# Layer 2 of the first expert placed between the parts of its layer 1, the first sigmoid one step later, and a pad tile, in an mLSTM cell followed by hash-routed experts

## The chip, the cores and the metric

The kernel runs on one core of one Trainium2 chip. The metric is the time of one execution on the device, in microseconds (us). Before the change three runs gave 402.64, 405.05 and 405.24 us; the median is 405.05 us. The engines are PE (matmul), ACT, DVE and POOL, and SP, whose queue issues most transfers.

## The reference

Two blocks follow each other, all in fp32. The first is an mLSTM cell over 4 batches, 8 heads, 768 positions and head dimension 40; the kernel computes it in chunks of 128 positions. The second sends each of the 3072 resulting rows of 320 numbers to one of 8 experts, picked by a hash of its token.

```python
m_new = np.maximum(f_gate[:, :, t] + m, i_gate[:, :, t])
f_stab = np.exp(f_gate[:, :, t] + m - m_new)
i_stab = np.exp(i_gate[:, :, t] - m_new)
C = f_stab[..., None, None] * C + i_stab[..., None, None] * np.einsum('bhd,bhe->bhde', vt, kt)
n = f_stab[:, :, None] * n + i_stab[:, :, None] * kt
o = 1.0 / (1.0 + np.exp(-o_gate[:, :, t]))
y[:, :, t] = o * np.einsum('bhde,bhe->bhd', C, qt) / np.maximum(np.abs(nq), 1.0)
...
x = attn_out.transpose(0, 2, 1, 3).reshape(B * S, H * D)
expert_idx = token_ids * np.int64(2654435761) % np.int64(E)
for e in range(E):
    xe = x[expert_idx == e]
    out[expert_idx == e] = np.maximum(xe @ w1[e], 0.0) @ w2[e]
```

## The kernel before

**Stage 1** runs 24 steps, s = 0 to 23, one for each batch and chunk of 128 positions. All instructions are written out by hand in the order in which each engine runs them (`manual_schedule`), so an engine that waits holds up everything behind it. In step s the SP queue issues the gate rows R of step s+3, k and q of step s+5, v of step s+4, then the o-gate tiles that the table `o_at` (L658) puts into this step, and last the stores of finished rows to `x_rows` (`waiting`). k and q lie in six buffers each, `[128, 8, 64]` in fp32, of which 40 of every 64 numbers are loaded: one 160-byte piece for each partition and head, 256 bytes apart. v lies in rows of 164 bytes, og in rows of 160 bytes that follow each other without a gap. Each of these loads carries 160 KB.

On PE a step begins with the transposes of k and q of step s+2 (`turn`, L321), then come scores (L368), decays (L332), the state (L399) and the output (L420, L426). ACT takes the exponentials (L336) and copies (dec L346, add L403, kT and qT L322). The output gate is taken for eight tiles at once: `sig_at` (L656) puts three sigmoids behind steps 6, 12 and 17, each a table load, an activation over 2560 columns, and a table load back (L360, L336). The sigmoid reads eight og tiles, so it waits for the last of these eight loads, and the next exponentials wait behind it. In the step after a sigmoid the copies of kT and qT go to DVE. After a sigmoid POOL multiplies two tiles a step by their gate (L443, `gated`), and SP stores them one or two steps later (L766).

**Stage 2** works off the experts in order. Layer 1 (`layer1`, L841) goes through eight blocks of hidden units in four pairs; each block gives a tile `mh` in PSUM (four buffers), which DVE or ACT turns into h by a relu (L864, L866). Layer 2 (`layer2`, L882) gives for each of three row tiles a tile `zp` (L886), which ACT copies (L819) and POOL scatters to the output (L820). The rows of an expert are gathered by POOL (L108), transposed on PE (L833, L835), and copied to xT by DVE or ACT (L839, L837). A fourth, shared tile xr holds 32 remainder rows of each of four experts; its transposed form remT is copied by POOL into the last 32 columns of xT (L919).

For expert 0 layer 1 is split. Its first two row tiles are gathered and transposed within stage 1 (`early_turn`), and part 1 runs over their 256 columns (L956). Then come the third tile and the remainder (`turns(0)[2:]`, L957), then part 2 over columns 256 to 416 (L959), then the three tiles of layer 2 (L961). The weights of expert 0 are loaded in slices by SP in steps 17 to 23; those of experts 1 and 2 (W1 and W2, 2.5 MB each) are issued from ACT's queue by `one` (L944) within part 2, and those of the later experts by SP.

Of the kernel before, what the change touches and what calls it, by code (L numbers as in the profile page):

```python
# [8 lines left out]
F32 = mybir.dt.float32  # L9
# [8 lines left out]
P = 128  # L18
# [4 lines left out]
def kernel(  # L23
# [66 lines left out]
    def weights(src1, src2, wpool, w2pool, eng=None):  # L90
# [10 lines left out]
        return w1t, w1c, w2t  # L101

    xg0 = early.tile([P, NJ, DB * P], F32, name="xg0")
    xT0 = early.tile([P, DB, CAP], F32, name="xT0")
# [39 lines left out]
    with tc.tile_pool(name="gates", bufs=1) as gp, \  # L144
# [481 lines left out]
        def route_index():  # L626
# [18 lines left out]
            2: [lambda: route_iotas(0)], 3: [lambda: route_iotas(1), route_consts, route_parts], 4: [route_experts],  # L645
            5: [route_chosen], 8: [route_extra, route_masked], 9: [route_rank], 10: [route_slots], 11: [route_places],
            21: [route_index], 22: [route_tiles],
# [6 lines left out]
        for i, part in enumerate(slices_of(0)):  # L654
            pieces.setdefault((17, 18, 19, 20, 21, 22, 23)[i], []).append(part)
        sig_at = {6: 0, 12: 1, 17: 2}  # L656
        o_at = {}
        for i, j in enumerate((2, 2, 3, 3, 4, 4, 5, 5, 6, 7, 8, 8, 9, 10, 10, 11, 12, 13, 13, 14, 15, 15, 16, 16)):  # L658
            o_at.setdefault(j, []).append(i)
# [61 lines left out]
        for s in range(NT):  # L721
# [43 lines left out]
            for i in range(2):  # L765
                if ndone < s and ndone // NG <= nsig and s - 1 not in sig_at:  # L766
                    gated(ndone)
                    waiting.setdefault(min(s + 1 + (s < NT - B - 1), NT), []).append(ndone)
                    ndone += 1
# [111 lines left out]

    def layer2(w, h, n, idx, apart, between=lambda j: None):  # L882
        for j in range(n):
            zp = mps.tile([P, Dm], F32, name="zp")
# [11 lines left out]
    with tc.manual_schedule():  # L896
# [38 lines left out]
        for e in range(E):  # L935
# [8 lines left out]
            def one(_):  # L944
                if ahead:
                    ahead.pop(0)()
                if e == 0 and len(W) < 3:
                    load_weights(len(W), nc.scalar)

# [5 lines left out]
            if e == 0:  # L955
                layer1(W[0], xT0, h, 0, 2 * P)  # L956
                for piece in turns(0)[2:]:  # L957
                    piece()
            layer1(W[e], xTs[e], h, 2 * P if e == 0 else 0, CAP, one)  # L959
            nc.gpsimd.tensor_copy(hrem[g][:, i], h[:, :, NM:])  # L960
            layer2(W[e], h, NJ, cols_of(s_idx, e * NJ), True, after)  # L961
            if e + 3 < E:
# [3 lines left out]
    with tc.If(nx > 0):  # L966
        with tc.For_i(0, nx, 1) as k:
# [13 lines left out]
            layer1(w, xT, h, 0, P)  # L981
            layer2(w, h, 1, lambda j: gs[:, 1:2], False)

# [29 lines left out]
```

## Time and profile before

| | before |
|---|---|
| median of 3 runs | 405.05 us (402.64 to 405.24) |
| profiled execution, its own time | 406.89 us |
| its span, first to last instruction | 405.0 us |
| mean granted TensorE clock (1 is full) | 0.971 |
| PE busy | 372.7 us, 92% |
| DVE, ACT, POOL busy | 34%, 28%, 36% |
| share of the chain that ended last: PE, POOL, DMA | 66%, 9%, 6% |

The span is the time on the chip's engines; the profiled execution's own time lies 1.9 us above it. PE is busy in most of the span in both stages, but matmuls are pipelined and their busy time also grows when the clock falls, so single waits are read from the timeline. A DMA share of 1.00 means that the 16 DMA engines have, on average, something under way all the time.

### The profile page before, as it was taken

The numbers are of one execution on the slowest core, as the hardware profiler recorded it, in microseconds if no ns is written. First come the engines' busy times: TensorE is split into PE (matmuls) and PEld (weight loads), VectorE is DVE, ScalarE is ACT, GpSimd is POOL, SyncE is SP. The second block draws the span as 40 slices with busy tenths as digits, with TensorE's granted clock in tenths as the row PEclk, the third lists the DMA queues.
The fourth block names the chain that finished last, engine by engine and source line by source line (L and its number), as shares of the span: only waits on it lengthen the run. The fifth ranks groups of instructions, "written<-read, shape, count | busy, mean of one in ns | idle before, by whom it ended". The sixth has DMA issues, their size and how long they took to land.

```text
span 405.0 us, 7980 instructions
## 1 busy us (share of the span) xinstructions
PE 372.7 (92%) x3211; PEld 260.8 (64%) x3211; DVE 138.6 (34%) x355; ACT 113.0 (28%) x232; POOL 144.0 (36%) x247
## 2 busy tenths in 40 slices
PE   8598896999998878799999999999999999999992
PEld 7487774878887765676565575556565575575561
DVE  8646765697786852110201201101201201101100
ACT  5366446558557421111111101201110101101100
POOL 8342424887996446113115023013115021010020
PEclk9789996999999999699999999999999999999998
DMA  9799999999999943897183192053182000000000
GB/s 124 107 157 125 149 160 148 158 188 160 159 171 203 265 157 99 270 362 245 32 235 106 32 275 81 20 182 128 32 252 93 14 16 31 2 32 16 2 18 31
DMA packets 124220, 51.02 MB, mean 126 GB/s; under 512 B 104338, under 2 KB 120174, under 8 KB 124182
## 3 DMA queue, kind: packets, MB, share of 16 engines
q1 hardware_dynamic: 116614, 36.73, 46.0%
q0 software_dynamic: 2496, 8.20, 6.5%
q10 hardware_dynamic: 5072, 5.57, 4.6%
q8 instruction: 26, 0.43, 0.5%
q14 instruction: 12, 0.10, 0.1%
HBM read 42.10 MB, written 8.71 MB: 125 GB/s over the span
## 4 chain that ended last, share of the span: by engine, by line
PE 66%; POOL 9%; issue 6%; DMA 6%; DVE 6%; ACT 5%; POOLq 0%; SPq 0%; DVEq 0%; ACTq 0%
PE zp L886 22%; PE mh L857 21%; PE mh L850 6%; PE tr L321 3%; PE sp L368 3%; DMA R<-gate_pieces 2%; PE xh L426 2%; POOL xg L108 2%; ACT og L360 2%; PE ab L332 2%; POOL x L443 1%; PE tp L833 1%; DVE w L374 1%; PE xh L420 1%; PE zp L927 1%
## 5 line engine op out<-in xcount | busy, mean ns | idle before, releaser
L886 PE MATMUL zp<-w2t,h 128*128 128x320 f32 x384 | 105.2, 433 | 0.0
L857 PE MATMUL mh<-xT,w1t 128*128 128x416 f32 (+2 forms) x288 | 98.6, 488 | 3.9 <-POOL xT L919 2.6
L886 PEld LDWEIGHTS zp<-w2t,h 128*128 128x128 f32 x384 | 72.7, 190 | 31.8 <-issue 2.9
L857 PEld LDWEIGHTS mh<-xT,w1t 128*128 128x128 f32 x288 | 52.6, 195 | 42.6 <-issue 38.0
L820 POOL DMA_INDIRECT out_dram<-zo,s_idx x26 | 25.6, 985 | 93.1 <-ACT zo L819 93.1
L839 DVE COPY xT<-tp 128x384 f32<-128x384 f32 x15 | 8.4, 558 | 139.1 <-PE tp L835 99.5
L866 ACT ACTIVATE h<-mh 128x416 f32<-128x416 f32 (+2 forms) x36 | 17.2, 478 | 113.3 <-PE mh L850 60.5
L864 DVE TENSOR_SCALAR h<-mh 128x416 f32<-128x416 f32 (+2 forms) x36 | 19.6, 543 | 60.1 <-PE mh L850 29.0
L819 ACT COPY zo<-zp 128x320 f32<-128x320 f32 x26 | 11.1, 425 | 101.6 <-PE zp L886 93.4
L374 DVE TENSOR_TENSOR w<-sp,w 128x512 f32<-128x512 f32 x48 | 30.8, 683 | 18.6 <-ACT w L336 18.6
L426 PE MATMUL xh<-v,w 128*64 128x41 f32 x768 | 34.8, 223 | 0.0
L336 ACT ACTIVATE w<-ab 128x512 f32<-128x512 f32 x48 | 26.0, 594 | 20.5 <-PE ab L332 17.9
L960 POOL COPY hrem<-h 128x256 f32<-128x256 f32 x8 | 3.2, 398 | 79.3 <-ACT h L866 79.3
L368 PE MATMUL sp<-qT,kT 64*128 64x128 f32 x384 | 30.4, 297 | 1.0 <-DVE w L374 0.9
L426 PEld LDWEIGHTS xh<-v,w 128*64 128x64 f32 x768 | 30.8, 139 | 0.1
L368 PEld LDWEIGHTS sp<-qT,kT 64*128 64x128 f32 x384 | 25.5, 199 | 5.4 <-issue 3.0
L850 PE MATMUL mh<-xT,w1c 64*128 64x416 f32 (+2 forms) x144 | 28.1, 509 | 0.4 <-DVE h L864 0.4
L108 POOL DMA_INDIRECT xg<-x_rows,g_idx x24 | 23.4, 974 | 13.2 <-issue 6.4
L420 PE MATMUL xh<-C,qs 128*64 128x82 f32 x320 | 27.4, 250 | 0.0
L409 POOL TENSOR_TENSOR C<-C,add 64x164 f32<-64x164 f32 x32 | 17.6, 551 | 26.9 <-ACT add L403 25.7
L321 PE MATMUL tr<-ident,q 128*128 128x128 f32 x96 | 15.8, 290 | 8.9 <-ACT dec L346 6.5
L443 POOL TENSOR_TENSOR x<-x,og 128x320 f32<-128x320 f32 x24 | 20.5, 872 | 5.4 <-DVE x L439 5.4
(188 smaller groups left out, 392.9 us busy)
## 6 DMA issues: line engine op xcount, KB each, us to landing
w2t<-in_moe_w_dram SPq DMA_DIRECT2D x5, 1280.0 KB
w1t<-in_moe_w_dram SPq DMA_DIRECT2D x5, 1024.0 KB
k<-in_k_dram SPq DMA_DIRECT2D x24, 160.0 KB
v<-in_v_dram SPq DMA_DIRECT2D x24, 160.0 KB
og<-in_o_gate_dram SPq DMA_DIRECT2D x24, 160.0 KB
x_rows<-x SPq DMA_DIRECT2D x24, 160.0 KB
q<-in_q_dram SPq DMA_DIRECT2D x23, 160.0 KB
w2t<-in_moe_w_dram ACTq DMA_DIRECT2D x2, 1280.0 KB
```

The source lines that it names most:

```text
L108: nc.gpsimd.indirect_dma_start(out=xg, out_offset=None, in_=x_d[:rows, :], in_offset=bass.IndirectOffsetOnAxis(ap=idx, axis=0),)
L321: nc.tensor.transpose(tp[:, j, :], d[what][:, 2 * j : 2 * j + 2, :].rearrange("p h d -> p (h d)"), ident[:])
L336: nc.scalar.activation(w[:, hf], ab[:], AF.Exp)
L368: nc.tensor.matmul(sp[hf][:, j, :], lhsT=d["kT"][r, j, :], rhs=d["qT"][r, j, :], start=True, stop=True)
L374: nc.vector.tensor_tensor(d["w"][:, hf], d["sp"][hf][:], d["w"][:, hf], op=ALU.mult)
L420: nc.tensor.matmul(xh[t, 2 * j : 2 * j + 2, :], lhsT=d["qs"][:, j, t], rhs=Cs[b][c % 2][:, j].rearrange("p h d -> p (h d)"), start=True, s ...
L426: nc.tensor.matmul(hs[t, 2 * j + hf, :], lhsT=d["w"][:, hf, j, t], rhs=d["v"][:, 2 * j + hf, :], start=(c == 0), stop=True, skip_group_che ...
L443: nc.gpsimd.tensor_tensor(x[:], x[:], og[s // NG][:, s % NG], op=ALU.mult)
L820: ins = nc.gpsimd.indirect_dma_start(out=out[:, :], out_offset=bass.IndirectOffsetOnAxis(ap=idx, axis=0), in_=zo[:], in_offset=None, bound ...
L850: nc.tensor.matmul(hp[i][:, : c1 - c0], lhsT=w1c[r, fp, :], rhs=xT[r, 2, c0:c1], start=first, stop=not first,)
L857: nc.tensor.matmul(hp[i][:, : c1 - c0], lhsT=w1t[:, db, fb * P : (fb + 1) * P], rhs=xT[:, db, c0:c1], start=(first and db == 0), stop=(not ...
L886: nc.tensor.matmul(zp[:], lhsT=h[:, fb, j * P : (j + 1) * P], rhs=w[2][:, fb, :], start=(fb == 0), stop=(fb == FB - 1),)
```

## The change

1. **Pad.** A tile of 128 bytes for each partition stands ahead of xg0 in the pool `early`. All that is laid out behind it moves by 128 bytes: xg0, xT0, h0, and the buffers of stage 1 and of stage 2. The first of the k and q buffers begin 224 bytes behind a multiple of 256 before and 96 bytes behind one after; with heads 256 bytes apart this holds for each of their 160-byte pieces. Before, a piece therefore has 32 bytes ahead of the next multiple and 128 behind it; after, it ends at the multiple. Of og's eight pieces in a row four cross such a multiple before and after.
2. **First sigmoid.** `sig_at` puts it behind step 7 instead of 6, and the first eight og loads move one step later. The routing pieces of step 8 move to step 7. Gating starts one step later, and rows are always stored in the step after their gating, so that tiles 8 and up are stored one step earlier than before.
3. **Layer 2 of expert 0.** Its tiles 0 and 1, whose columns of h are complete after part 1, now run behind part 1; the third row tile and the remainder are transposed between them (behind tile 0). The loads of W1 and W2 are issued on ACT within part 1.

```diff
+    early.tile([P, 32], F32, name="pad")
     xg0 = early.tile([P, NJ, DB * P], F32, name="xg0")
...
-            5: [route_chosen], 8: [route_extra, route_masked], 9: [route_rank], 10: [route_slots], 11: [route_places],
+            5: [route_chosen], 7: [route_extra, route_masked], 9: [route_rank], 10: [route_slots], 11: [route_places],
...
-        sig_at = {6: 0, 12: 1, 17: 2}
+        sig_at = {7: 0, 12: 1, 17: 2}
         o_at = {}
-        for i, j in enumerate((2, 2, 3, 3, 4, 4, 5, 5, 6, 7, 8, 8, 9, 10, 10, 11, 12, 13, 13, 14, 15, 15, 16, 16)):
+        for i, j in enumerate((3, 3, 4, 4, 5, 5, 6, 6, 7, 8, 8, 9, 9, 10, 10, 11, 13, 13, 14, 14, 15, 15, 16, 16)):
...
-                    waiting.setdefault(min(s + 1 + (s < NT - B - 1), NT), []).append(ndone)
+                    waiting.setdefault(s + 1, []).append(ndone)
...
-    def layer2(w, h, n, idx, apart, between=lambda j: None):
-        for j in range(n):
+    def layer2(w, h, js, idx, apart, between=lambda j: None):
+        for j in js:
...
             def one(_):
                 if ahead:
                     ahead.pop(0)()
-                if e == 0 and len(W) < 3:
-                    load_weights(len(W), nc.scalar)
...
-                layer1(W[0], xT0, h, 0, 2 * P)
-                for piece in turns(0)[2:]:
-                    piece()
+                layer1(W[0], xT0, h, 0, 2 * P, lambda fp: len(W) < 3 and load_weights(len(W), nc.scalar))
+                third = turns(0)[2:]
+                layer2(W[0], h, range(2), cols_of(s_idx, 0), True, lambda j: j == 0 and [piece() for piece in third])
             layer1(W[e], xTs[e], h, 2 * P if e == 0 else 0, CAP, one)
...
-            layer2(W[e], h, NJ, cols_of(s_idx, e * NJ), True, after)
+            layer2(W[e], h, range(2 if e == 0 else 0, NJ), cols_of(s_idx, e * NJ), True, after)
```

PE between the two stages before, from the end of part 1 (128x256) over part 2 (128x160) to layer 2 of expert 0 (xT_72 is xT0, h_73 is h0):

```order
L850 MATMUL mh<-xT_72,w1c 128x256 x4
L857 MATMUL mh<-xT_72,w1t 128x256 x4
L833 MATMUL tp<-ident,xg_71 128x128 x2
L835 MATMUL tp<-ident,xg_71 128x128
L833 MATMUL tp<-ident,xr 128x128 x2
L835 MATMUL tp<-ident,xr 128x128
L857 MATMUL mh<-xT_72,w1t 128x160 x4
...
L850 MATMUL mh<-xT_72,w1c 128x160 x4
L857 MATMUL mh<-xT_72,w1t 128x160 x4
L886 MATMUL zp<-w2t,h_73 128x320 x24
```

The same place after (names one higher, lines shifted by one):

```order
L851 MATMUL mh<-xT_73,w1c 128x256 x4
L858 MATMUL mh<-xT_73,w1t 128x256 x4
L887 MATMUL zp<-w2t,h_74 128x320 x8
L834 MATMUL tp<-ident,xg_72 128x128 x2
L836 MATMUL tp<-ident,xg_72 128x128
L834 MATMUL tp<-ident,xr 128x128 x2
L836 MATMUL tp<-ident,xr 128x128
L887 MATMUL zp<-w2t,h_74 128x320 x8
L858 MATMUL mh<-xT_73,w1t 128x160 x4
...
L851 MATMUL mh<-xT_73,w1c 128x160 x4
L858 MATMUL mh<-xT_73,w1t 128x160 x4
L887 MATMUL zp<-w2t,h_74 128x320 x8
```

Eight matmuls of layer 2 now stand ahead of the transposes and eight between them and part 2; eight are left behind part 2.

ACT at the same place before; the relus of 256 columns are part 1, those of 160 part 2:

```order
L665 COPY xT_72<-tpx 128x3x128 x2
L866 ACTIVATE h_73<-mh 128x256 x4
L837 COPY remT<-tp 128x384
L96 DMA w1t<-in_moe_w_dram 128x2x1024
L99 DMA w1c<-in_moe_w_dram 64x4x128 x2
L100 DMA w2t<-in_moe_w_dram 128x8x320
L866 ACTIVATE h_73<-mh 128x160 x2
```

And after:

```order
L666 COPY xT_73<-tpx 128x3x128 x2
L96 DMA w1t<-in_moe_w_dram 128x2x1024
L99 DMA w1c<-in_moe_w_dram 64x4x128 x2
L100 DMA w2t<-in_moe_w_dram 128x8x320
L867 ACTIVATE h_74<-mh 128x256 x2
L96 DMA w1t<-in_moe_w_dram 128x2x1024
L99 DMA w1c<-in_moe_w_dram 64x4x128 x2
L100 DMA w2t<-in_moe_w_dram 128x8x320
L867 ACTIVATE h_74<-mh 128x256 x2
L820 COPY zo<-zp 128x320
L838 COPY remT<-tp 128x384
```

Both weight loads have moved ahead of relus of part 1, the first of them ahead of all.

SP in steps 15 and 16 before, up to the last two o-gate tiles:

```order
L192 DMA v_101<-in_v_dram 128x8x40
L188 DMA og<-in_o_gate_dram 128x8x40 x2
L202 DMA R_122<-gate_pieces 6x2x1024
L192 DMA k_91<-in_k_dram 128x8x40
L192 DMA q_96<-in_q_dram 128x8x40
L192 DMA v_102<-in_v_dram 128x8x40
L209 DMA L_117<-gate_pieces 8x4x128 x3
L188 DMA og<-in_o_gate_dram 128x8x40 x2
L446 DMA x_rows<-x 128x320 x2
```

And after:

```order
L193 DMA v_102<-in_v_dram 128x8x40
L189 DMA og<-in_o_gate_dram 128x8x40 x2
L447 DMA x_rows<-x 128x320 x2
L203 DMA R_123<-gate_pieces 6x2x1024
L193 DMA k_92<-in_k_dram 128x8x40
L193 DMA q_98<-in_q_dram 128x8x40
L193 DMA v_103<-in_v_dram 128x8x40
L210 DMA L_118<-gate_pieces 8x4x128 x3
L189 DMA og<-in_o_gate_dram 128x8x40 x2
```

One pair of stores (tiles 8 and 9) now stands ahead of the last two o-gate tiles.

## Rows read from the trace of the kernel before

**Rows 1.** Windows: busy time of each engine, granted clock, DMA share, GB/s.
```profile
60.00:80.00 20.00, 15.32 (x233) 12.77 (x234) 10.85 (x28) 12.19 (x23) 12.39 (x24) 0.83 1.16 151
100.00:120.00 20.00, 19.75 (x386) 16.88 (x384) 16.14 (x41) 9.60 (x23) 18.92 (x30) 1.00 1.03 169
```

**Rows 2.** Timeline, PE: transposes of k, which begin steps 8, 9, 10, 12, 13, 19 and 20.
```profile
59.43 0.66 PE L321 MATMUL tr<-ident,k 128*128 128x128 f32 x4
...
71.85 0.66 PE L321 MATMUL tr<-ident,k 128*128 128x128 f32 x4
...
76.68 0.66 PE L321 MATMUL tr<-ident,k 128*128 128x128 f32 x4
...
87.34 0.66 PE L321 MATMUL tr<-ident,k 128*128 128x128 f32 x4
...
92.88 0.62 PE L321 MATMUL tr<-ident,k 128*128 128x128 f32 x4
...
123.23 0.66 PE L321 MATMUL tr<-ident,k 128*128 128x128 f32 x4
...
130.29 0.66 PE L321 MATMUL tr<-ident,k 128*128 128x128 f32 x4
```

**Rows 3.** Timeline, ACT: ahead of the first, second and third sigmoid; in brackets idle time.
```profile
53.65 0.29 ACT L403 COPY add<-xh 128x164 f32<-128x164 f32 x1
58.63 1.28 ACT L360 ACT_TABLE_LOAD   x1 [4.69 <-DMA R<-gate_pieces]
...
91.74 1.28 ACT L360 ACT_TABLE_LOAD   x1
...
119.57 1.28 ACT L360 ACT_TABLE_LOAD   x1 [2.38 <-DMA x_rows<-x]
```

**Rows 4.** Windows: each ends when a k, q, v and og load of 160 KB has landed.
```profile
84.70:85.68 0.98, 0.44 (x16) 0.47 (x17) 0.91 (x5) 0.81 (x2) 0.55 (x1) 1.00 1.36 153
85.68:86.79 1.11, 1.11 (x43) 1.11 (x40) 1.08 (x4) 0.00 (x0) 0.57 (x1) 1.00 1.50 159
86.79:87.77 0.98, 0.98 (x25) 0.93 (x22) 0.98 (x3) 0.38 (x2) 0.90 (x3) 1.00 1.41 231
87.77:88.33 0.56, 0.56 (x7) 0.42 (x4) 0.56 (x3) 0.30 (x1) 0.56 (x2) 1.00 0.93 314
```

**Rows 5.** Timeline, SP's queue: the stores behind the last o-gate tiles.
```profile
117.00 1.33 SPq L446 DMA_DIRECT2D x_rows<-x  x2
```

**Rows 6.** Timeline, PE, from part 1's end to expert 1.
```profile
157.16 1.99 PE L857 MATMUL mh<-xT,w1t 128*128 128x256 f32 x8
...
161.39 0.33 PE L835 MATMUL tp<-ident,xr 128*128 128x128 f32 x1 [1.65 <-DVE xg L834]
...
164.33 2.50 PE L857 MATMUL mh<-xT,w1t 128*128 128x160 f32 x8 [2.61 <-POOL xT L919]
...
173.62 1.35 PE L857 MATMUL mh<-xT,w1t 128*128 128x160 f32 x8
...
174.81 7.43 PE L886 MATMUL zp<-w2t,h 128*128 128x320 f32 x27
...
187.73 2.61 PE L857 MATMUL mh<-xT,w1t 128*128 128x416 f32 x7
```

**Rows 7.** Windows, as group 1: part 2 of layer 1.
```profile
166.00:168.00 2.00, 2.00 (x11) 1.63 (x11) 0.50 (x1) 0.00 (x0) 0.00 (x0) 0.50 0.99 388
```

**Rows 8.** Timeline, ACT: first relu of part 1, and the issues of W1.
```profile
152.20 0.38 ACT L866 ACTIVATE h<-mh 128x256 f32<-128x256 f32 x1 [5.15 <-PE mh L850]
...
163.48 0.40 ACTq L96 DMA_DIRECT2D w1t<-in_moe_w_dram  x1
...
165.24 0.61 ACTq L100 DMA_DIRECT2D w2t<-in_moe_w_dram  x1
```

**Rows 9.** The chain that ended last: a gather and the last store of stage 1.
```profile
142.97 2.91 DMA xg<-x_rows,g_idx
...
150.31 1.75 DMA x_rows<-x
```

More of the change, by code (lines that the diff above doesn't have):

```diff
@@ L981 @@
             layer1(w, xT, h, 0, P)
-            layer2(w, h, 1, lambda j: gs[:, 1:2], False)
+            layer2(w, h, range(1), lambda j: gs[:, 1:2], False)
 _INS = ['q', 'k', 'v', 'i_gate', 'f_gate', 'o_gate', 'moe_token_ids', 'moe_w1', 'moe_w2']
```

## The prediction

> **What bounds the kernel now.** I read the windows of 20 us first, then PE's steps in the timeline, then what ACT and PE wait for at the two places that the change touches. In stage 1 the DMA engines are full: a share of 1.16 in 60 to 80 us and 1.03 in 100 to 120 us, at only 151 and 169 GB/s [rows 1]. PE is busy for 19.75 of 20 us in the second of these windows and for 15.32 in the first, where its granted clock is 0.83. So stage 1 runs along two limits that lie close together. A step of PE with nothing in its way takes 76.68 - 71.85 = 4.83 us [rows 2]; the step in which the first sigmoid blocks ACT takes 71.85 - 59.43 = 12.42 us. ACT has nothing to do from 53.94 us and begins the sigmoid at 58.63, after 4.69 us [rows 3]. The releaser printed there is a later R load, but the sigmoid reads og alone: so I take the last og loads to be what it waits for. At the second sigmoid ACT goes on without idling, and that step takes 92.88 - 87.34 = 5.54 us. At the third it idles 2.38 us, and the step takes 130.29 - 123.23 = 7.06 us. A sigmoid thus costs PE 0.7 us when og is there, 7.6 when it is 4.7 us late, 2.2 when it is 2.4 us late.
>
> The second place is the bridge. Part 1 of layer 1 ends at 157.16 + 1.99 = 159.15 us; part 2 begins at 164.33 [rows 6]. In between PE has six transposes (1.65 and 2.61 us of its idle time carry names there), and what ends last is the chain of copies on DVE, ACT and POOL that fills xT. PE comes back with a clock of 0.50 [rows 7]: eight matmuls of 160 columns take 2.50 us at 164.33 and 1.35 us at 173.62. From expert 1 on PE is busy without a gap until the tail, and the change leaves the order there alone.
>
> **Part A: the first sigmoid.** The eight og loads and the sigmoid both move one step, so SP has one more R, k, q and v ahead of the last og. If transfers are as long as before, that is about 0.3 + 0.98 + 1.11 + 0.98 = 3.4 us (0.3, an estimate, for the small R; the others are the windows of [rows 4]), while ACT comes one step of 4.83 us later. The wait falls from 4.69 to 4.69 + 3.4 - 4.83 = 3.3 us: a gain of about 1.4 us, some 2 with the clock that it keeps up. But it isn't kept. The stores of tiles 8 and 9 now stand ahead of the last og pair of the third sigmoid; such a pair held SP for 1.33 us [rows 5]. With full DMA engines all the way, og 23 lands 1.3 us later, whatever ACT gained at step 7. Without a change to the transfers, stage 1 ends about 1.3 us later.
>
> **Part B: the pad.** The diff says nothing of its effect, and I take it as the largest term. Four loads of 160 KB, landing one behind the other, take 0.98 us (k), 1.11 (q), 0.98 (v) and 0.56 (og), at 153, 159, 231 and 314 GB/s [rows 4]. They have the same size, pieces (160 bytes) and source layout; what differs is where the pieces lie in SBUF. All of k's and q's cross a multiple of 256 bytes, five in eight of v's, four in eight of og's, and the slow ones are those that cross most. After the pad none of k's and q's do. So a k or q load should fall from 1.05 us (the mean of the two) toward 0.56, by up to 0.5 us. The window of og has a DMA share of 0.93 and what other queues moved in it counts too, so the difference may be flattered: ends are 0 and 0.5 us, and I take 0.25, half of it, since og in turn still crosses with half of its pieces.
>
> The Trainium skill, page "DMA: Bandwidth & Descriptors", section "How a descriptor splits into AXI transactions", says that a transaction starts at a multiple of 256 bytes, so that a piece which begins ahead of one needs an extra transaction. By that rule a piece of k or q needs two before and one after; were time to go by transactions alone, the load would halve, to 0.5 us by rows 4. The trace agrees in the order of the loads but not in their sizes: by the rule og's pieces need 1.5 transactions on average, so that k would take a third longer than og (an estimate), and rows 4 show nearly twice.
>
> What does 0.25 us buy? Ahead of og 7 lie some ten k and q loads since the DMA engines filled up (steps 2 to 6): 2.5 us, against a wait of 3.3 us, so 0.8 us remains. That step then costs like the second sigmoid's (0.7 over a normal one) plus 0.8: the gain is 7.6 - 1.5 = 6.1 us. Up to og 23 there are 30 such loads (steps 2 to 16): 7.5 us, less 1.3 for the two stores, 6.2 us earlier, while ACT comes 6.1 us earlier: the third wait stays near 2.3 us, and 0.1 us is gained there. Steps 14 to 17 are held by POOL, busy for 18.92 of 20 us [rows 1], and give nothing. Stage 1: **-6.2 us**. At 0.5 us a load both waits vanish and the gain is bounded by compute: 7.6 - 0.7 at the first, 2.2 - 0.7 at the third, 8.4 us. At nothing: +1.3 us.
>
> **Part C: the bridge.** All in times of before. The first zp follows at 159.15. Three zp tiles took 187.73 - 174.81 = 12.92 us, so one takes 4.3 us: until 163.45. xr had landed before its last transpose ran at 161.39 us [rows 6], so both gathered tiles are there. The six transposes take 1 us, with the wait for DVE's copy of xr's last columns inside (1.65 us in before, [rows 6]); I take 1.2 of it, since DVE no longer waits for a gather. At 165.65 zp 1 follows, until 169.95, and under it lie the copies to remT and xT, which took the 2.61 us that PE waited. Part 2 starts at 170.0 instead of 164.33. It took 10.48 us (164.33 to 174.81). Its first eight long matmuls fall from 2.50 to 1.35, and the others of the first half (to about 170 us) by the same measure less: together some 2.4 us at a clock that doesn't fall, 8.1 us are left, until 178.1. The last zp ends at 182.4 instead of 187.73: -5.3 us. I take off 0.3 us for the relus in part 1 that now wait behind two weight loads on ACT: **-5.0 us**. If the clock falls all the same, -2.6; with no wait for the copy and xr, -6.5.
>
> Hidden: the issue of W1, four entries from 163.48 to 165.85 [rows 8], 2.4 us, and as much for W2. The relu of 152.20 comes behind the first of them, at about 154.5; its buffer is wanted again by the second block of the third of four pairs, about 4 us ahead of the end at 159.15 by the pace of the last eight long matmuls (1.99 us), near 155.2. W1 itself, 2.5 MB, is wanted at 182 us and has 25 us. The moved routing pieces lie on POOL and DVE in a step in which neither bounds.
>
> **Sum.** -6.2 - 5.0 = -11.2 us from a span of 405.0, thus 393.8. The profiled execution's own time was 406.89, 1.9 above its span, and the median 405.05, so medians come out near the span: 405.05 - 11.2 = 393.85, **393.9 us**.
>
> **Rivals.**
> - **The pad changes no transfer.** For it: v's 0.98 us lies near k's although fewer of its pieces cross, and a load that lands last in a batch may profit from idle queues. Against it: og's 0.56. Then +1.3 - 5.0 = -3.7: 401.3 us.
> - **The stall moves behind the transposes.** W1 and W2 are under way while the gathers of xg and xr run, and xr lands late; zp 1 then waits, and the clock falls there. A gather among stage 1's transfers took 2.91 us [rows 9]. xr was there by 161.39 and is now wanted at 163.45, so it would have to land 2 us later, which only a gather of nearly twice that length does; this speaks against it. If it happened, the bridge would give 2 us only: 405.05 - 6.2 - 2.0 = 396.9 us.
> - **Slower: the pad lengthens k and q.** One mechanism, at SP's loads: should the layout before be the better one, each 0.1 us more a load lengthens a stage whose DMA engines are full by 3.0 us. With the 1.3 us of the stores, and 5.0 us saved at the bridge, the kernel is slower from 3.7 / 30 = 0.12 us a load on; at 0.25 it would be 405.05 + 1.3 + 7.5 - 5.0 = 408.9 us. Nothing in [rows 4] speaks for it.
> - **Slower part 1.** W1's first load needs memory of stage 1, which is free when the last store lands, 150.31 + 1.75 = 152.06 us [rows 9]. From a delay of 0.7 us on, PE waits in part 1. A delay of 2 us would cost 1.3 us, and with a fall of the clock as in [rows 7] some 3: it lessens the gain, 393.9 + 3 = 396.9 us.
>
> **How the numbers follow.** Forecast (the pad helps by 0.1 to 0.5 us a load, the bridge gives 4 to 6.5): 0.62, from 390.1 (gains of 8.4 + 6.5) to 399.3 us (3.0 - 1.3 + 4.0). No effect of the pad: 0.23, 400 to 402.5. A stall that moves, or a slower part 1, with a helpful pad: 0.10, 395 to 399 us. Slower: 0.05. For 8 in 10 the range goes from 390 to 402 us. One per cent, about what a measurement of this kernel can tell from no change, is 4 us: faster means under 401.0. The first and third case lie there, and a third of the second: 0.80. Same: the rest of the second, 0.15. Slower: 0.05.
>
> **What would show it.** Pad: in windows that end with landings of k and q, over 180 GB/s instead of 153 to 159; a DMA share below 1.0 in 60 to 100 us. First sigmoid: idle under 1 us ahead of its table load, a step of under 7 us in place of 12.42, no clock of 0.83. Third: idle of 1 to 2 us; over 3 means that transfers are as they were. Bridge: part 2 begins 10 to 11 us after part 1's end instead of 5.2, at a clock of 1.00, and expert 1 begins 23.3 us after it instead of 28.6. The prediction is wrong if k and q loads still take 1.05 us, or if PE idles over 2.5 us between the two zp.

## The result

The changed kernel takes 388.84 us (median of 4 runs, 388.61 to 388.96), the kernel before took 405.14 us beside it: a ratio of 0.961, with a 95% interval of 0.957 to 0.965. That is 16.3 us less. The forecast was 393.9 us with a range from 390.0: the direction was right, the time lies 1.2 us below the range. Two later comparisons of the same pair, on other chips, gave 0.968 [0.963, 0.973] and 0.961 [0.957, 0.965]; there the changed kernel took 391.24 and 391.61 us, inside the range. Among all runs below one, of b_pad with 402.07 us, was in a slower state; its ratio leaves this run out, and the median of its other three is 394.99 us.

The profiled execution's span is 386.7 us, against 405.0: 18.3 us less. That is more than the medians show, since the profiled execution of before, at 406.89 us, was 1.8 us above its median. From the first matmul of expert 1 to the last instruction it is 217.27 us in both, and in every trace of this study. So all of it comes from ahead of expert 1, 11.9 us from stage 1 and 6.4 us from the bridge (from the start of part 1 to expert 1):

| start of | before, us | after, us | gained so far | gained in this stretch | forecast |
|---|---|---|---|---|---|
| PE's step 0 | 17.14 | 15.71 | 1.43 | 1.4 | 0 |
| step 8 | 59.43 | 56.78 | 2.65 | 1.2 | 0 |
| step 10, behind the first sigmoid | 76.68 | 67.26 | 9.42 | 6.8 | 6.1 |
| step 19 | 123.23 | 114.18 | 9.05 | -0.4 | 0 |
| step 20, behind the third sigmoid | 130.29 | 119.00 | 11.29 | 2.2 | 0.1 |
| part 1 of layer 1 | 149.48 | 137.60 | 11.88 | 0.6 | 0 |
| expert 1 | 187.73 | 169.46 | 18.27 | 6.4 | 5.0 |

The windows of the changed kernel that answer to [rows 1] (busy time of PE, PEld, DVE, ACT, POOL; granted clock, DMA share, GB/s):

```profile
60.00:80.00 20.00, 18.45 (x356) 15.87 (x354) 15.86 (x40) 11.83 (x27) 14.87 (x29) 1.00 1.00 192
...
100.00:120.00 20.00, 19.88 (x385) 17.07 (x382) 16.63 (x40) 13.78 (x26) 17.79 (x29) 1.00 0.99 232
```

In 60 to 80 us the share has come down from 1.16 to 1.00 and the rate up from 151 to 192 GB/s; PE is busy for 18.45 us in place of 15.32, and its granted clock is 1.00 in place of 0.83. PE's timeline, transposes of k that begin steps 8, 9, 10, 19 and 20, as in [rows 2]:

```profile
56.78 0.66 PE L322 MATMUL tr<-ident,k 128*128 128x128 f32 x4
...
61.61 0.66 PE L322 MATMUL tr<-ident,k 128*128 128x128 f32 x4
...
67.26 0.66 PE L322 MATMUL tr<-ident,k 128*128 128x128 f32 x4
...
114.18 0.66 PE L322 MATMUL tr<-ident,k 128*128 128x128 f32 x4
...
119.00 0.66 PE L322 MATMUL tr<-ident,k 128*128 128x128 f32 x4
```

The step that holds the first sigmoid, now step 9, takes 67.26 - 61.61 = 5.65 us, where the blocked one took 12.42. The third sigmoid's step takes 4.82 us instead of 7.06. ACT's table loads ahead of the three sigmoids have no idle time in brackets, where [rows 3] had 4.69 and 2.38 us ahead of the first and the third:

```profile
56.14 1.28 ACT L361 ACT_TABLE_LOAD   x1
...
82.69 1.28 ACT L361 ACT_TABLE_LOAD   x1
...
108.16 1.28 ACT L361 ACT_TABLE_LOAD   x1
```

Windows that end with the landings of a k, q, v and og load, as in [rows 4] (the first also holds what came between the loads of two steps):

```profile
56.60:57.72 1.12, 1.12 (x18) 0.99 (x14) 0.95 (x5) 1.11 (x2) 0.97 (x3) 1.00 0.39 66
57.72:58.40 0.68, 0.68 (x12) 0.60 (x12) 0.68 (x2) 0.68 (x1) 0.68 (x2) 1.00 1.15 204
58.40:59.33 0.93, 0.93 (x15) 0.63 (x14) 0.82 (x2) 0.93 (x1) 0.44 (x1) 1.00 1.00 180
59.33:60.18 0.85, 0.85 (x26) 0.75 (x23) 0.40 (x1) 0.84 (x2) 0.00 (x0) 1.00 1.14 205
```

q lands 0.68 us behind k, where it took 1.11. Over all loads of q between 33 and 125 us of the span the median from landing to landing is 0.70 us after (16 loads) and 1.07 before (16). v stays near where it was (1.03 after, 0.98 before), and og, half of whose pieces cross a multiple in both kernels, went from 0.71 to 0.92. So a time from landing to landing holds more than the load's own crossings, and q's difference is not all net gain.

The start gains too. PE's wait for k ahead of step 0, before and after:

```profile
17.14 1.09 PE L321 MATMUL tr<-ident,k 128*128 128x128 f32 x4 [3.21 <-DMA k<-in_k_dram]
```

```profile
15.71 1.09 PE L322 MATMUL tr<-ident,k 128*128 128x128 f32 x4 [1.74 <-DMA k<-in_k_dram]
```

The bridge, PE and POOL, as in [rows 6]:

```profile
144.21 1.91 PE L851 MATMUL mh<-xT,w1c 64*128 64x256 f32 x8
...
145.19 0.98 POOL L109 DMA_INDIRECT xg<-x_rows,g_idx  x1 [6.79 <-PE mh L851]
...
146.05 1.99 PE L858 MATMUL mh<-xT,w1t 128*128 128x256 f32 x8
...
147.88 4.47 PE L887 MATMUL zp<-w2t,h 128*128 128x320 f32 x16
...
152.19 0.38 PE L834 MATMUL tp<-ident,xg 128*128 128x128 f32 x2
...
153.22 0.41 PE L834 MATMUL tp<-ident,xr 128*128 128x128 f32 x2 [0.54 <-issue]
...
153.62 4.47 PE L887 MATMUL zp<-w2t,h 128*128 128x320 f32 x16
...
157.93 1.25 PE L858 MATMUL mh<-xT,w1t 128*128 128x160 f32 x8
...
165.15 4.47 PE L887 MATMUL zp<-w2t,h 128*128 128x320 f32 x16
...
169.46 2.96 PE L858 MATMUL mh<-xT,w1t 128*128 128x416 f32 x8
```

The first zp begins as part 1 ends; the transposes and their waits take 5.74 us from zp to zp, less the 4.31 us of a zp (174.81 to 179.12 in the trace of before): 1.43 us. Part 2 begins without a wait and takes 7.38 us to its last matmul's end, where it took 10.65. Its clock, for [rows 7]:

```profile
158.00:160.00 2.00, 2.00 (x20) 1.83 (x18) 0.45 (x1) 0.43 (x1) 1.16 (x2) 1.00 0.07 24
```

### The profile page after: what moved, and what is told of

Its sections match the earlier page's. It is cut to its first block, busy times and chain, and to the rows that moved or that the text cites. A ratio compares the mean times of both kernels' runs of the same rounds, so it can differ in the third digit from the quotient of the medians.

```text
span 386.7 us, 7979 instructions
## 1 busy us (share of the span) xinstructions
PE 366.6 (95%) x3211; PEld 255.7 (66%) x3211; DVE 138.0 (36%) x355; ACT 113.0 (29%) x232; POOL 143.8 (37%) x247
## 4 chain that ended last, share of the span: by engine, by line
PE 77%; DVE 8%; issue 6%; POOL 3%; ACT 2%; SPq 2%; DMA 1%; POOLq 0%; DVEq 0%; ACTq 0%
PE mh L858 24%; PE zp L887 23%; PE mh L851 7%; PE sp L369 5%; PE tr L322 5%; PE xh L427 3%; PE ab L333 2%; PE xh L421 2%; PE xh L400 2%; PE tp L834 1%; DVE w L375 1%; PE zp L928 1%; POOL out_dram L821 1%; SPq L193 1%; SPq L189 1%
## 5 line engine op out<-in xcount | busy, mean ns | idle before, releaser
L858 PE MATMUL mh<-xT,w1t 128*128 128x416 f32 (+2 forms) x288 | 97.0, 481 | 1.3 <-DVE x L440 1.3
L858 PEld LDWEIGHTS mh<-xT,w1t 128*128 128x128 f32 x288 | 51.3, 190 | 39.8 <-issue 37.8
L375 DVE TENSOR_TENSOR w<-sp,w 128x512 f32<-128x512 f32 x48 | 30.8, 682 | 10.7 <-ACT w L337 10.7
L369 PE MATMUL sp<-qT,kT 64*128 64x128 f32 x384 | 29.5, 291 | 1.7 <-DVE w L375 0.9
L369 PEld LDWEIGHTS sp<-qT,kT 64*128 64x128 f32 x384 | 24.7, 193 | 6.0 <-issue 2.8
L851 PE MATMUL mh<-xT,w1c 64*128 64x416 f32 (+2 forms) x144 | 27.9, 497 | 0.1
L355 POOL TENSOR_TENSOR kw<-k,kwT 128x320 f32<-128x320 f32 x20 | 14.4, 723 | 13.1 <-DMA q<-in_q_dram 7.7
```

Source lines behind the costliest of these rows:

```text
L369: nc.tensor.matmul(sp[hf][:, j, :], lhsT=d["kT"][r, j, :], rhs=d["qT"][r, j, :], start=True, stop=True)
L375: nc.vector.tensor_tensor(d["w"][:, hf], d["sp"][hf][:], d["w"][:, hf], op=ALU.mult)
L851: nc.tensor.matmul(hp[i][:, : c1 - c0], lhsT=w1c[r, fp, :], rhs=xT[r, 2, c0:c1], start=first, stop=not first,)
L858: nc.tensor.matmul(hp[i][:, : c1 - c0], lhsT=w1t[:, db, fb * P : (fb + 1) * P], rhs=xT[:, db, c0:c1], start=(first and db == 0), stop=(not ...
```

## Experiments

Theory 1: the pad shortens each load of k and q, because their pieces no longer cross a multiple of 256 bytes, and that frees stage 1. Theory 2: the new order of og loads and sigmoids frees it. Beside them stands the bridge, with its own question: what of its gain is the covered wait, and what the clock.

In the table, stage 1 is where part 1 begins, the bridge goes from there to expert 1; both are from each run's trace. The medians were compared with the kernel before on the same chip, so the ratios are what compares across groups.

| run | median, us | ratio to before [95%] | stage 1 | bridge |
|---|---|---|---|---|
| before (first trace) | 405.05 | 1 | 149.48 | 38.25 |
| changed (first trace) | 388.84 | 0.961 [0.957, 0.965] | 137.60 | 31.86 |
| a_nopad | 403.03 | 0.991 [0.988, 0.994] | 152.81 | 31.83 |
| b_pad | 395.68 | 0.973 [0.968, 0.978] | 139.32 | 36.60 |
| b_sig | 409.27 | 1.008 [1.004, 1.013] | 153.68 | 38.38 |
| b_bridge | 400.25 | 0.985 [0.981, 0.990] | 150.00 | 31.83 |
| a_pad256 | 404.12 | 0.995 [0.993, 0.998] | 152.25 | 32.76 |
| a_pad160 | 404.24 | 0.994 [0.992, 0.996] | 151.89 | 31.82 |
| a_pad96 | 391.53 | 0.965 [0.962, 0.968] | 140.14 | 32.26 |
| a_kcross | 394.36 | 0.972 [0.969, 0.974] | 142.42 | 32.58 |
| after_again | 391.24 | 0.968 [0.963, 0.973] | 140.52 | 32.15 |
| b_pad_bridge | 390.24 | 0.966 [0.962, 0.970] | 140.37 | 31.82 |
| a_Wlate | 391.99 | 0.969 [0.965, 0.974] | 141.09 | 31.74 |
| b_filled | 404.43 | 0.999 [0.996, 1.003] | 150.71 | 34.62 |
| after_third | 391.61 | 0.961 [0.957, 0.965] | 140.60 | 32.52 |
| c_og25 | 390.99 | 0.962 [0.958, 0.966] | 138.62 | 31.95 |
| c_og5 | 390.95 | 0.961 [0.956, 0.965] | 139.26 | 32.46 |
| c_og2 | 390.16 | 0.958 [0.954, 0.962] | 138.93 | 32.29 |

### One part at a time

**a_nopad**: the changed kernel less its pad.

```diff
-    early.tile([P, 32], F32, name="pad")
     xg0 = early.tile([P, NJ, DB * P], F32, name="xg0")
```

> The changed kernel without its pad tile: first sigmoid behind step 7 and layer 2 in the bridge as in the changed kernel, k and q again 224 bytes behind a multiple of 256. Theory 1 (the pad shortens each k and q load, and that frees stage 1): a k or q load takes 1.05 us or more again, the first sigmoid waits about 3 us and the third over 3 us, stage 1 ends 0 to 1.5 us later than in the kernel before, and only the bridge's 6.4 us are left: 398.5 to 400.5 us. Theory 2 (the new order of the og loads and sigmoids frees stage 1, the pad does nothing): within 1 us of 388.8 us.

**b_pad**: the same line added to the kernel before.

```diff
+    early.tile([P, 32], F32, name="pad")
     xg0 = early.tile([P, NJ, DB * P], F32, name="xg0")
```

> The kernel before with the pad tile alone. Theory 1: loads of k and q fall by some 0.45 us each; the first sigmoid, still behind step 6, waits under 1 us, the third not at all, and stage 1 ends 9 to 12 us sooner: 393 to 396 us. Theory 2: 404 to 406 us. A third way, that pad and order are needed together: the first sigmoid still waits 2 to 3 us, 397 to 400 us.

**b_sig**: the edits of `pieces`, `sig_at`, `o_at` and `waiting` in the kernel before.

```diff
-        sig_at = {6: 0, 12: 1, 17: 2}
+        sig_at = {7: 0, 12: 1, 17: 2}
...
-                    waiting.setdefault(min(s + 1 + (s < NT - B - 1), NT), []).append(ndone)
+                    waiting.setdefault(s + 1, []).append(ndone)
```

> The kernel before with the move of the first sigmoid, the og loads, the routing pieces and the stores alone (no pad, no layer 2 in the bridge). Theory 1: the first sigmoid's wait falls to about 3 us, but the third's grows by as much, since the loads are the limit: 403.5 to 406.5 us. Theory 2: 393 to 395 us.

**b_bridge**: the edits of `layer2` and of the weight loads in the kernel before.

```diff
...
-                layer1(W[0], xT0, h, 0, 2 * P)
-                for piece in turns(0)[2:]:
-                    piece()
+                layer1(W[0], xT0, h, 0, 2 * P, lambda fp: len(W) < 3 and load_weights(len(W), nc.scalar))
+                third = turns(0)[2:]
+                layer2(W[0], h, range(2), cols_of(s_idx, 0), True, lambda j: j == 0 and [piece() for piece in third])
...
```

> The kernel before with the move of layer 2 and of the weight loads alone. Both theories: stage 1 as before, the bridge about 6.4 us shorter (from the end of part 1 to expert 1 22.2 us in place of 28.6): 398 to 399.5 us. If the bridge gains only because stage 1 frees the queues sooner, less: 401 us or more.

Measured, against 406.62 us of before on that chip: the pad alone gives about 11 us (10.9 by the median in the table, 11.6 by that of its other three runs), the bridge alone 6.4 us, the move of the sigmoid alone costs 2.7 us. Without the pad the changed kernel takes 403.03 us, only 3.6 us less than before; it is slower than the bridge alone by 2.8 us, which is again the price of the moved sigmoid. Theory 2 is out and theory 1 holds. a_nopad and b_sig came out 2.5 and 2.8 us above the bands of theory 1, since the move cost more than the 0 to 1.5 us allowed for it, and the chip's kernel before was 1.5 us slower; b_bridge came out 0.75 us above its band. ACT's first and third table loads in a_nopad and in b_sig:

```profile
62.55 1.28 ACT L360 ACT_TABLE_LOAD   x1 [5.35 <-DMA og<-in_o_gate_dram]
...
121.70 1.28 ACT L360 ACT_TABLE_LOAD   x1 [5.00 <-DMA og<-in_o_gate_dram]
```

```profile
62.01 1.28 ACT L360 ACT_TABLE_LOAD   x1 [3.09 <-DMA og<-in_o_gate_dram]
...
121.24 1.28 ACT L360 ACT_TABLE_LOAD   x1 [5.49 <-DMA og<-in_o_gate_dram]
```

The first wait falls only in b_sig, to 3.09 us; in a_nopad, whose stage 1 runs the same program, it is 5.35, longer than the 4.69 of before. The third wait grows in both, to 5.0 and 5.5 us in place of 2.38. That the pair of stores ahead of the last og adds to it is likely, but no run moves the stores alone. In b_pad, with the first sigmoid still behind step 6, the first wait is nearly gone and the other two are; in b_pad_bridge, whose stage 1 runs the same program on another chip, the first is 2.09 us:

```profile
51.99 1.28 ACT L361 ACT_TABLE_LOAD   x1 [0.48 <-DMA k<-in_k_dram]
```

```profile
53.32 1.28 ACT L361 ACT_TABLE_LOAD   x1 [2.09 <-DMA og<-in_o_gate_dram]
```

The start goes with the pad: over all traces PE's wait for k ahead of step 0 is 2.97 to 3.27 us where pieces of k and q cross, and 1.74 to 2.46 where none does (2.63 in a_kcross, below).

### Where a piece lies against multiples of 256 bytes

**a_pad256**, **a_pad160**, **a_pad96**: the pad's size in the changed kernel, 64, 40 and 24 numbers of 4 bytes; the diff is that of the first.

```diff
-    early.tile([P, 32], F32, name="pad")
+    early.tile([P, 64], F32, name="pad")
```

> The changed kernel with a pad of 256 bytes in place of 128: k and q lie 224 bytes behind a multiple of 256 again, though a pad is there. If the place against multiples of 256 decides (theory 1): as without a pad, 398.5 to 400.5 us. If any shift of the buffers helps (another tile's address, a bank): near 388.8 us.

> The changed kernel with a pad of 160 bytes: k and q pieces begin 128 bytes behind a multiple of 256, so each crosses the next multiple after 128 bytes and has 32 behind it, the mirror of the layout before. If crossing decides: 398 to 401 us, as without a pad. If a start at a multiple of 128 or 64 bytes decides: near 388.8 us.

> The changed kernel with a pad of 96 bytes: k and q pieces begin 64 bytes behind a multiple of 256 and end ahead of the next, crossing none. If crossing decides: within 1 us of 388.8 us, the pad of 128 bytes is one of several that serve. If the end of a piece at a multiple decides: slower, 394 us or more.

**a_kcross**: the pad between the k and the q buffers.

```diff
-    early.tile([P, 32], F32, name="pad")
...
         ks = [gp.tile([P, H, DP], F32, name=f"k{i}") for i in range(KV)]
+        gp.tile([P, 32], F32, name="pad")
         qs = [gp.tile([P, H, DP], F32, name=f"q{i}") for i in range(KV)]
```

> The changed kernel with the pad tile moved between the k and the q buffers: k's pieces cross a multiple of 256 as before, q's and all behind them lie as in the changed kernel. If each crossing load costs some 0.45 us (theory 1): k loads near 1.0 us and q loads near 0.65 us; stage 1 loses part of its gain: half of it if loads are the limit throughout (394 us), less if compute has become the limit with half the gain (390 to 392 us). If the pad acts on something else than the load itself: 388.8 or 400 us, and k and q equal.

A pad of 256 bytes, which leaves the place against 256 as it was, gives 404.12 us, one of 160, with a crossing at 128 of 160 bytes, 404.24 us; both stand with no pad at all (403.03 us; ratios 0.991 to 0.995), some 3 to 4 us above the bands named for a crossing, which allowed too little for the move of the sigmoid. A pad of 96 bytes, with pieces that cross nothing and end ahead of the multiple, gives 391.53 us: more than 388.8, but like what the changed kernel took on other chips (391.24, 391.61), and its ratio, 0.965, lies between theirs. So neither a shift as such nor an end at the multiple matters, only the crossing. The median from landing to landing of the q loads goes with it: 1.07 us in the kernel before, 1.11 without a pad, 1.10 at 256 and 1.09 at 160, but 0.70 with the pad and 0.70 at 96.

With k crossing and q not, 394.36 us, between. The windows that end with a k and a q landing in a_kcross:

```profile
67.73:68.62 0.89, 0.89 (x35) 0.89 (x32) 0.89 (x3) 0.63 (x3) 0.89 (x2) 1.00 1.34 197
68.62:69.30 0.68, 0.68 (x23) 0.63 (x19) 0.61 (x2) 0.00 (x0) 0.68 (x2) 1.00 1.36 210
```

q takes 0.68 us there (median 0.63 over 16 loads), k 0.89 (0.96), beside each other and of one size. k comes behind the small R load, so its window is less clean than q's. By its number 394.36 us is the case of loads that are the limit throughout, but beside a_pad96 on the same chip only about 3 us of the 12 come back when half of the loads cross again, and not 6. That compute is already close to being the limit with the other half gone fits this, but isn't shown; no run lets q alone cross, and the pad also moves v and all that lies behind it.

### What the sigmoid's move and the weight loads are worth, and the clock

**after_again** is the changed kernel itself. **b_pad_bridge** is the changed kernel without the edits of b_sig.

> The changed kernel itself, so that the runs sent with it can be compared with it on one chip: 0.960 of the kernel before, 388 to 391 us by the chip.

> The changed kernel without the move of the first sigmoid (with the pad and with layer 2 in the bridge). If the move adds to the pad (the first sigmoid behind step 6 still finds its last og late): 2 to 4 us slower than the changed kernel. If the pad alone has made the og loads early enough: within 0.5 us of the changed kernel, and the move is worth nothing. If the move only costs, as it does alone (2.7 us slower than before): 1 to 3 us faster.

**a_Wlate** issues W1 and W2 within part 2 again.

```diff
                 if ahead:
                     ahead.pop(0)()
+                if e == 0 and len(W) < 3:
+                    load_weights(len(W), nc.scalar)
...
-                layer1(W[0], xT0, h, 0, 2 * P, lambda fp: len(W) < 3 and load_weights(len(W), nc.scalar))
+                layer1(W[0], xT0, h, 0, 2 * P)
```

> The changed kernel with the loads of W1 and W2 back in part 2, as in the kernel before. If the early weight loads delay the last store and the gathers and with them the transposes behind the first zp: the gathers start 5 us sooner against part 1, PE's idle time between the two zp (1.2 us) falls by 0.5 to 1 us, and the kernel is 0.5 to 1 us faster. If the late loads come back as relus that wait in part 2 or as weights that come late for expert 1 (wanted 24 us behind part 1): 0 to 3 us slower.

**b_filled** puts matmuls without a use into the idle time of the bridge of before.

```diff
                 for piece in turns(0)[2:]:
                     piece()
+                idle = mps.tile([P, Dm], F32, name="zp")
+                for _ in range(16):
+                    nc.tensor.matmul(idle[:, :P], lhsT=ident[:], rhs=ident[:], start=True, stop=True)
```

> The kernel before with 16 matmuls on the identity (128 columns, results unused) behind the transposes of the bridge, where PE waits for xT: they fill its idle time and change nothing else. If the bridge loses time to the clock besides the wait: part 2 begins as before, at a clock near 1.00, and takes 8 us in place of 10.5: 2 to 2.5 us faster than before. If the slow clock comes from something else than the idle time, or costs nothing: within 0.5 us of before, or slower by what the matmuls take.

On one chip the changed kernel took 391.24 us, without the sigmoid's move 390.24, with the late weights 391.99; their intervals overlap. With the pad in place the move is worth nothing that can be measured, in either direction. Nothing measurable comes from the early weight loads either. In a_Wlate the end of part 1, the transposes between the two zp and the late part of part 2 read:

```profile
147.71 1.14 PE L851 MATMUL mh<-xT,w1c 64*128 64x256 f32 x8
148.77 2.00 PE L858 MATMUL mh<-xT,w1t 128*128 128x256 f32 x8
...
156.15 0.33 PE L836 MATMUL tp<-ident,xr 128*128 128x128 f32 x1 [0.54 <-DVE xr L835]
...
166.86 0.54 PE L851 MATMUL mh<-xT,w1c 64*128 64x160 f32 x4 [0.41 <-DVE h L865]
```

From zp to zp, less the zp itself, PE needs 1.41 us here, 1.43 in the changed kernel's first trace and 1.73 in after_again, on a_Wlate's chip. The gathers do start 4.2 us sooner in a_Wlate, but then DVE's copy of xr's last columns comes last, for as long a wait.

Part 1 takes 9.67 us, as before, and 10.44 in the changed kernel, where the eight matmuls of L851 at 144.21, shown above, take 1.91 us in place of 1.14. Part 2 takes 8.06 us in place of 7.38. So the weight issues cost about 0.7 us on whichever part they stand in. It isn't that relus wait behind them: ACT's third relu begins 7.39 us behind part 1's start in both kernels. The changed kernel's chain that ended last goes through DVE's third relu there, which in a_Wlate PE doesn't wait for:

```profile
144.28 0.68 PE mh L851 x4
144.97 0.42 DVE h L865
145.38 0.04 issue
145.43 0.70 PE mh L851 x2
```

Why the place of the issues makes PE wait for it is open.

b_filled's median can't be told apart from before. Its trace shows the bridge 3.6 us shorter, with part 2 at full clock from its start:

```profile
162.00:164.00 2.00, 2.00 (x21) 2.00 (x20) 0.00 (x0) 0.34 (x1) 1.69 (x3) 1.00 0.62 145
164.00:166.00 2.00, 2.00 (x19) 2.00 (x18) 0.00 (x0) 0.00 (x0) 0.26 (x2) 1.00 1.02 383
```

```profile
165.20 1.25 PE L857 MATMUL mh<-xT,w1t 128*128 128x160 f32 x8
```

The gap ahead of part 2 is 4.82 us (before 5.17), and part 2 takes 7.38 us (before 10.65). So within the trace the idle time costs 3.3 us behind it, by the clock of 0.50 that [rows 7] shows and that is 1.00 here. The 2 to 2.5 us expected of the whole kernel did not come: by the medians it is 0.6 us, and the interval of the ratio (0.996 to 1.003) leaves room for less than 2. That the trace's 3.3 us don't show in the median is left open: stage 1 of this one trace ended 1.2 us later than in the first trace of before, and the kernel before itself went from 402.43 to 407.66 us on that chip.

### Is the first sigmoid's wait gone?

The changed kernel's stage 1 ended at 137.60 us in its first trace and near 140.5 in the two others. In after_again ACT and PE show this at the first sigmoid (61.34 and 70.63 begin steps 9 and 10):

```profile
58.02 1.28 ACT L361 ACT_TABLE_LOAD   x1 [2.16 <-DMA og<-in_o_gate_dram]
```

```profile
61.34 0.66 PE L322 MATMUL tr<-ident,k 128*128 128x128 f32 x4
...
64.56 0.66 PE L322 MATMUL tr<-ident,q 128*128 128x128 f32 x4 [2.56 <-ACT dec L347]
...
70.63 0.66 PE L322 MATMUL tr<-ident,k 128*128 128x128 f32 x4
```

The last og of the first eight is still late there by 2.16 us, and the step takes 70.63 - 61.34 = 9.29 us, where the first trace had 5.65. a_Wlate, with the same stage 1, waits 2.73 us. Three kernels issue these loads earlier.

The first eight entries of `o_at` become 2, 2, 3, 3, 4, 4, 5, 5 in c_og25, 3, 3, 4, 4, 4, 5, 5, 5 in c_og5 and 2, 3, 3, 4, 4, 5, 5, 6 in c_og2; the diff is that of c_og25. after_third is the changed kernel.

```diff
-        for i, j in enumerate((3, 3, 4, 4, 5, 5, 6, 6, 7, 8, 8, 9, 9, 10, 10, 11, 13, 13, 14, 14, 15, 15, 16, 16)):
+        for i, j in enumerate((2, 2, 3, 3, 4, 4, 5, 5, 7, 8, 8, 9, 9, 10, 10, 11, 13, 13, 14, 14, 15, 15, 16, 16)):
```

> The changed kernel once more, as the reference for the runs sent with it: 0.958 to 0.970 of the kernel before. If its first sigmoid waits 2 us for og again in the profile, stage 1 ends near 140.5 us, else near 137.6.

> The changed kernel with the first eight og loads issued in steps 2 to 5, as in the kernel before, while the first sigmoid stays behind step 7. If what is left of stage 1's loss is the first sigmoid's wait for og (2.2 us in one profile of the changed kernel, nothing in another, and a clock that falls behind it): no wait at any sigmoid, 0 to 3 us faster than the changed kernel beside it. If loads moved ahead of k, q and R only shift the wait: steps 4 to 6 grow by as much, no gain, or up to 1 us slower.

> The changed kernel with the first eight og loads in steps 3, 3, 4, 4, 4, 5, 5, 5: nothing of them in step 2, where the queue still fills, and one step of room ahead of the sigmoid. If the wait for og is what is left: 0 to 3 us faster than the changed kernel, as the run with steps 2 to 5 or better. If three loads in one step hold k, q and R up: steps 6 and 7 grow, no gain.

> The changed kernel with the first eight og loads in steps 2, 3, 3, 4, 4, 5, 5, 6: one of them earlier than in the changed kernel, the last still in step 6. If the last og decides, and one load of room (0.9 us) is too little: between the changed kernel and the run with steps 2 to 5.

In all three traces the first table load has no idle time ahead of it, as here in c_og25, while after_third beside them waits 2.02 us:

```profile
57.20 1.28 ACT L361 ACT_TABLE_LOAD   x1
```

Stage 1 ends at 138.62 to 139.26 us, 1.3 to 2.0 us sooner than after_third. The medians lie 0.6 to 1.5 us below its 391.61, with intervals that overlap: the wait goes, but what it is worth is too little for these runs to show. after_third, which waits again, also ends stage 1 at 140.60 us, as expected of that case. c_og2, at 390.16 us, has the lowest ratio, 0.958 [0.954, 0.962]; no version is shown to beat the changed kernel.

## Why the prediction was right or wrong

**Direction and mechanism of the pad: right.** It was named as the largest term, and it is: about 11 us alone, beside 6.4 for the bridge. The price of a crossing came from the right place, the difference between loads in [rows 4], and the rule of the Trainium skill, page "DMA: Bandwidth & Descriptors", section "How a descriptor splits into AXI transactions", gave the right line between pads that work and pads that don't: 128 and 96 bytes do, 0, 160 and 256 don't. Counted in transactions it doesn't give the size: two in place of one don't double the load, 1.07 us goes to 0.70.

**Where the sum fell short.** By the spans the gain was 18.3 us and the forecast 11.2. Of the 7.1 us between them 2.65 were gained at the start, 2.4 at the sigmoids and the steps between them, 0.6 behind the third sigmoid and 1.4 at the bridge.

**The first step that failed is the size of the pad's term.** I took 0.25 us a load, half of the bound of 0.5; the runs show 0.37 to 0.46 for q (1.07, 1.11, 1.10, 1.09 us crossing, 0.70, 0.70, 0.69 and 0.63 not). With 0.25 the sum left the third sigmoid a wait of 2.3 us and gave it a gain of 0.1; that wait is gone in all traces of the changed kernel, and its step gives 2.2 us. The halving was argued from og, which crosses with half of its pieces; that argument works the other way: if half of og's pieces cross and it lands faster, a load with none should land faster still. The og window of 0.56 us was too short, as suspected: over all 24 loads its median was 0.71 before and 0.92 after.

With 0.4 us instead of 0.25, the forecast's own sum gives 30 x 0.4 - 1.3 = 10.7 us as far as loads reach, above the 8.4 us that it allowed when both waits vanish. Both did vanish in the first trace: 6.8 us at the first sigmoid (forecast 6.1) and 2.2 at the third (forecast 0.1), 9.0 together, 8.6 with the 0.4 us that the steps between gave back.

At the first sigmoid that was in part luck. In the three other traces with this stage 1 (after_again, after_third, a_Wlate) it still waits 2.0 to 2.7 us, and its stretch gains 1.5 to 3.2 us, about half of the forecast or less. There stage 1 ends about 3 us later than in the first trace, and these runs' medians (391.2 to 392.0 us) lie inside the range. Why the wait comes and goes is open; the 1.2 us by which the time came out below the range are less than these 3 us.

**The second step that failed is the start, which the sum put at nothing.** 2.65 us are gained ahead of step 8, and 2.9 to 3.7 in those three traces; b_pad and b_pad_bridge, with the og loads where they were before, gain 2.4 and 2.7. PE's wait for the first k that lands late was 3.21 us before and 1.74 after; loads of k and q fill the queue there, and nothing in the trace of before excludes a gain. The range reached down to 390.1 only because it took sigmoids for the only places where stage 1 waits.

**The first sigmoid's move: right that it isn't kept without the pad,** and too low in price: 1.3 us was forecast, 2.7 measured (b_sig; 2.8 from a_nopad to b_bridge). Its first half, a wait of 3.3 us in place of 4.69, holds in b_sig (3.09) and fails in a_nopad (5.35). With the pad it was taken to matter, and no difference is measured: b_pad_bridge took 390.24 us, the changed kernel 391.24 beside it, with intervals that overlap.

**The bridge: right mechanism, 1.4 us short.** Forecast 5.0, measured 6.4. Two terms were too small: the clock, 2.4 us forecast and 3.3 by the traces (10.65 to 7.38 us for part 2, with the clock at 1.00; b_filled shows the same 3.3 with no zp moved), and the transposes between the zp, 2.2 us forecast and 1.43 measured. One loss was put too low: for relus behind the weight loads 0.3 us were taken off, and part 1 takes 0.8 us more (10.44 us for 9.67; a_Wlate removes it), though, as shown above, by a wait for DVE's relu and not by late relus on ACT. The three make up 1.2 of the 1.4 us.

**The rival that the stall moves: its cause was there, at a small price.** I wrote that W1 waits for the last store of stage 1. It doesn't: ACT issues W1 at 136.37, ahead of that store, and both are then under way on the same DMA engines (share 1.05 from 138.42 to 144.41 us). The store, issued at 138.42, lands at 144.41, after 6.0 us instead of the 1.75 of [rows 9]; in a_Wlate it is 1.75 again. The gathers, which wait for it, begin 7.6 us behind part 1's start (145.19) in place of 3.3, and the third row tile is read by DVE at 151.93:

```profile
151.93 0.20 DVE L835 COPY xg<-xg 128x64 f32<-128x64 f32 x1 [4.29 <-DMA xg<-x_rows,g_idx]
```

The first zp ends at 152.19, a quarter of a microsecond later: the 4.3 us of layer 2 just hid 4.2 us of delay that the change itself had made. The gather behind it, of xr, was late: it lands 6.7 us after its issue at 146.47, and PE's 0.54 us ahead of the xr transposes at 153.22, shown above as "issue", end with it. In after_again the profile names it:

```profile
156.09 0.41 PE L834 MATMUL tp<-ident,xr 128*128 128x128 f32 x2 [0.33 <-DMA xr<-x_rows,g_idx]
```

In the first trace that cost nothing against a_Wlate (1.43 and 1.41 us from zp to zp), since there DVE's copy takes as long. In after_again the transposes and waits take 1.73 us, in after_third 2.09 and in a_pad256 2.34, and the bridge is 0.3, 0.7 and 0.9 us longer than in the first trace: far less than the 3 us that the rival forecast.

**The slower rivals** did not come. That the pad lengthens loads is excluded by b_pad, where q falls to 0.69 us. That W1 waits for memory of stage 1 and holds up part 1 did not happen: its issue ends before part 1's first relu.

## What to carry to other kernels

When a stage runs at a full DMA share and a low rate, look where each small piece of a load lies in the destination, and price a crossing by loads that differ only in that. A gain in the limit shows wherever something waits for it, the start included, so list every wait on the stage's transfers and not only the largest. Independent work put into PE's wait saved here the wait and, in the traces, the slow clock behind it; but what is started earlier by the same edit may delay the very input that was waited for. And a forecast that lands near one trace should be held against several: a wait of 2 us was there in three and gone in one.

## What the runs showed of the hardware that I had not expected

- A load of q, 1024 pieces of 160 bytes (160 KB), takes 0.63 to 0.70 us from landing to landing (medians) when no piece crosses a multiple of 256 bytes in the destination and 1.07 to 1.11 us when all do, whichever side the 32 bytes lie on (pads of 0 and 160 bytes).
- A store of 160 KB landed 1.75 us after its issue with the DMA engines at a share of 0.26, and 6.0 us after it, at a share of 1.05, behind 2.5 MB of weights that another queue had begun to issue 2 us earlier.
- 4.3 us of idle PE (1.65 and 2.61 us in [rows 6]) cost 3.3 us more behind them in the trace of before: 7.38 us of matmuls took 10.65, with a clock of 0.50 from 166 to 168 us. In b_sig and b_pad, with the same order, they took 10.81 and 9.68.
